# A Fourier filter and gated feed-forward kernel: the middle inverse stage with its operands exchanged, and its result passed on by crossbar transposes

## The chip, the cores and the metric

The kernel runs on one core of one Trainium2 chip. The core has five engines with queues of their own: TensorE (PE, with its weight loads listed apart as PEld), VectorE (DVE), ScalarE (ACT), GpSimd (POOL) and SyncE (SP, which here only issues DMAs). The metric is the time of one execution on the device in microseconds; lower is better. Several executions of one program are timed, and one more is profiled.

## The reference

The input x has 8 sequences of 3008 positions and 256 channels. Each sequence goes through a real Fourier transform along its positions, is multiplied by a complex filter for each frequency and channel, and is transformed back. The result, all 24064 rows of it, then goes through a feed-forward block: root-mean-square norm with a gain, two projections to 1536 columns, SiLU of one times the other, and a projection back to 256.

```python
X = np.fft.rfft(x, axis=1)
F = (filt_r + 1j * filt_i)[None, :, :]
y = np.fft.irfft(X * F, n=x.shape[1], axis=1)

rms = np.sqrt(np.mean(x * x, axis=-1, keepdims=True) + 1e-06)
xn = x / rms * rms_g
g = xn @ w_gate
silu = g * (1.0 / (1.0 + np.exp(-g)))
val = xn @ w_val
return (silu * val @ w_out).astype(np.float32)
```

Here `x` in the second part is y as rows of 256 channels. The output is float32; the kernel computes in fp16 with float32 sums.

## The kernel before

**The transform.** 3008 is 64 x 47, so the long transform is done in two stages each way, as small matrix products. Forward, stage A (`a_unit`) transforms over the 64 (n2), for two columns of n1 at a time; two halves of n1 (24 and 23 columns) lie in the two halves of the 128 partitions. Its result goes to DRAM (`z_store`, tensor z_tmp) and comes back with other axes on the partitions (`t2_load`). Stage B (`b_unit`) transforms over the 47, for two of the 32 values of k2 at a time. The product with the filter (lines 221, 241, 244 for batch 2 on; lines 234 and 235 for batches 0 and 1) gives tiles s of 128 frequencies' real and imaginary parts by 2 x 256 channels. From batch 2 on the two halves of the complex product are added on POOL (line 244) to one tile; in batches 0 and 1 two tiles are left, and the next matmul sums them.

**The middle inverse stage** is `bi_unit`: for each of the two k2, the matmul's stationary operand is a table wi of 128x128, the moving operand is s with 256 columns. It gives 96 useful rows (real and imaginary part for 48 columns of n1) on the partitions and channels along the free axis. ACT copies them to a tile t3 of four k2; `g_store` writes t3 to DRAM (g_tmp), and `t4_load` reads it back in four chunks of six n1 with 4 DMAs each, so that real and imaginary parts for 32 k2, and the two halves of n1, lie on the 128 partitions. 47 is odd: the last column of an even batch has only one half, so the odd batch after it takes the other half's row of the batch before (line 275), and both are computed together.

**The last stage** (`n_unit`) transforms over n2: the table wai is stationary, t4 moves. ACT copies the result and squares it (`sq_unit`), POOL makes the root (`stat_unit`) and scales (`xt_unit`), and `tr_unit` lays it out with channels on the partitions by a DMA transpose on SP's queue. Batch 0's first two groups of four columns take another way (`n_first`, `q_unit`, `scale_split`, `scale_apply`), with t4 as stationary operand.

**The feed-forward block.** For each batch there are 6 groups of 4 columns (512 rows; the last group of an even batch 3 columns), and for each group 12 slices of 128 hidden columns. `gv` makes four matmuls of 512 columns for a slice into the banks pg and pv, SiLU on ACT, the product on DVE; `down` makes four matmuls of 256 columns, two slots later.

**The order** is written out by hand, engine by engine in program order, by a table of slots: one slot is one `gv`, 72 slots a batch. `at(slot, ...)` places the units of the transforms of later batches between them. Batch 0's transform stands before the slots, in a loop of its own. For batch b of 3 on, with t = 72(b-1), `b_unit` i stands at t - 26 + 4i, `bi_unit` i at 8 slots later (`lag`), `t4_load` at t + 46 to t + 49, `n_unit` from t + 51 in steps of 4. Batch 1 has lag 3, loads at 53, rows from 55; batch 2 has lag 4, loads at 118, rows from 123. Each engine works its queue strictly in order, SP's queue of DMA issues included.

**PSUM.** The banks pg and pv are two each, po two; psa, psi and psn (lines 192, 253, 289) of batch 1 on share one bank (tag "mx"), psb has one. In batch 0 psi takes the pv banks.

**Buffers the change touches:** t3 (2 buffers), t4 (4), xt (2), sq (2), the table wi.

Of the kernel before, what the change touches and what calls it, by code (L numbers as in the profile page):

```python
# [11 lines left out]
FP16 = mybir.dt.float16  # L12
AXT = mybir.ActivationFunctionType
# [7 lines left out]
P = 128  # L21
D = 256
B = 8
DFF = 1536
JT = DFF // P
H = 24
K2 = 32
SL = 48
KR = 2 * SL
HALF = 64  # L30
S_INV_B = 0.25
S_INV_A = 0.25
# [6 lines left out]
def _make_tables():  # L39
# [18 lines left out]
    wb = np.zeros((KR, K2, P))  # L58
    wi = np.zeros((P, 1, 2, P))
    re, im = slice(0, N1), slice(SL, SL + N1)  # L60
# [36 lines left out]
    f = np.float16  # L97
    wi0 = wi[:, 0] * S_INV_B
    return wa.astype(f), (wai * S_INV_A).astype(f), wb.astype(f), wi0.astype(f), np.eye(P).astype(f)


@with_exitstack
def kernel(
# [12 lines left out]

    wa_np, wai_np, wb_np, wi0_np, id_np = _make_tables()
    wa_d = nc.inline_tensor(wa_np, name="wa_t").ap()
    wai_d = nc.inline_tensor(wai_np, name="wai_t").ap()
    wb_d = nc.inline_tensor(wb_np, name="wb_t").ap()  # L120
    wi0_d = nc.inline_tensor(wi0_np, name="wi0_t").ap()
    id_d = nc.inline_tensor(id_np, name="id_t").ap()

    z_d = nc.dram_tensor("z_tmp", (B, K2, KR, D), FP16, kind="Internal").ap()
    g_d = nc.dram_tensor("g_tmp", (B, K2, KR, D), FP16, kind="Internal").ap()

# [5 lines left out]
    ssp = ctx.enter_context(tc.tile_pool(name="ssp", bufs=3))  # L132
    t3p = ctx.enter_context(tc.tile_pool(name="t3p", bufs=2))
    t4p = ctx.enter_context(tc.tile_pool(name="t4p", bufs=4))
# [16 lines left out]
    wb = glob.tile([KR, K2, P], FP16)  # L151
    wi = glob.tile([P, K2, 2, P], FP16)
    fr = [glob.tile([P, KC, D], FP32, name="fr%d" % c) for c in range(K2 // KC)]
# [9 lines left out]

    st = {b: {"x": {}, "t1": {}, "t2": {}, "s": {}, "t3": {}, "t4": {}, "y": {}, "sq": {},
              "u": {}, "xn": {}} for b in range(B)}
# [81 lines left out]
    def bi_unit(b, i):  # L247
        ss = st[b]["s"].pop(i)
        ps = bank(0 if b else 2, "psi").rearrange("p (a d) -> p a d", a=2)
        n = len(ss)  # L250
        for u in range(2):
            for q in range(n):
                nc.tensor.matmul(ps[:, u, :], wi[:, 2 * i + u, q, :], ss[q][:, u, :],  # L253
                                 start=(q == 0), stop=(q == n - 1))
        c, r = divmod(i, 2)
        if r == 0:
            st[b]["t3"][c] = t3p.tile([KR, 4, D], FP16, tag="t3", name="t3")
        nc.scalar.activation(out=st[b]["t3"][c][:, 2 * r:2 * r + 2, :], in_=ps[0:KR], func=AXT.Copy)  # L258

    def g_store(b, c):  # L260
        nc.sync.dma_start(g_d[b, 4 * c:4 * c + 4, :, :].rearrange("k p d -> p k d"),
                          st[b]["t3"].pop(c))

    def t4_load(b, c):
        t = t4p.tile([P, XC, D], FP16, tag="t4", name="t4")
        w = XC - 1 if c == NXC - 1 else XC
        for h in range(2):
            for ri in range(2):
                p0 = h * 64 + ri * 32
                r0 = ri * SL + h * H + c * XC  # L270
                wh = XC if (b % 2 and not h) else w
                (nc.scalar if b == 0 and c == 0 and h else nc.sync).dma_start(
                    t[p0:p0 + 32, 0:wh, :], g_d[b, :, r0:r0 + wh, :])
                if wh < XC and b % 2:
                    nc.sync.dma_start(t[p0:p0 + 32, wh, :], g_d[b - 1, :, ri * SL + H - 1, :])
        st[b]["t4"][c] = t
# [51 lines left out]
    def n_first(m):  # L328
        y = yp.tile([P, 2, 512], FP32, tag="y", name="y")
        sq = sqp.tile([P, 2, 512], FP16, tag="sq", name="sq")  # L330
        for dh in range(2):
# [127 lines left out]
    def wi_group(g):  # L459

        ps = bank(1 + g % 2, "pst").rearrange("p (a d) -> p a d", a=4)
        lo = 1 if g == 0 else 0
        for a in range(lo, 4):
            nc.tensor.matmul(ps[:, a, :], wb[:, 4 * g + a, :], ident[0:KR, :], start=True, stop=True)
        k = slice(4 * g + lo, 4 * g + 4)
        nc.scalar.activation(out=wi[:, k, 0, :], in_=ps[:, lo:4, :], func=AXT.Copy, scale=S_INV_B)
        for p0 in (0, HALF):
            nc.vector.tensor_scalar(out=wi[p0:p0 + HALF, k, 1, :],
                                    in0=ps[HALF - p0:P - p0, lo:4, :], scalar1=S_INV_B,
                                    scalar2=None, op0=ALU.mult)  # L470
# [29 lines left out]
    with tc.manual_schedule():  # L500
# [3 lines left out]
        for c in range(NXC):  # L504
            x_load(0, c)
        nc.sync.dma_start(wa, wa_d)
        nc.sync.dma_start(ident, id_d)
        wb_load(0)
# [33 lines left out]
        for i in range(19):  # L542
# [9 lines left out]
            if i >= 3:  # L552
                bi_unit(0, i - 3)
                if i % 2 == 0:
                    g_store(0, i // 2 - 2)
            if i == 16:
# [36 lines left out]
        for b in range(1, B):  # L593
# [5 lines left out]
            elif b == 2:  # L599
                a_at = [22 + 2 * i for i in range(12)]  # L600
                b_at = [50 + 4 * i for i in range(16)]
                lag, t4_at, n_at = 4, 118, 123
            else:
# [9 lines left out]
            for i in range(16):  # L613
# [5 lines left out]
                at(s0 + lag, bi_unit, b, i)  # L619
                if i % 2 == 1:  # L620
                    at(s0 + lag + 1, g_store, b, i // 2)
            if b + 1 < B:
# [52 lines left out]
```

## Time and profile before

Three executions took 949.34 to 952.16 us, median 950.18. The profiled execution:

| what | value |
| --- | --- |
| its time | 950.33 us |
| its span, first to last instruction | 948.5 us |
| mean granted TensorE clock | 0.962 |
| matmuls po (line 415), 2256 | 343.5 us, 272 ns each |
| matmuls pg and pv (line 398), 2304 | 676.8 us, 375 ns each |
| matmuls psi (line 253), 320 | 272 ns each at full clock |
| ACT copies of psi (line 258), 128 | 75.6 us, 593 ns each |
| POOL sums s (line 244), 96 | 110.7 us, 1153 ns each |
| g_tmp stores, 64 of 192 KB | 2.7 us from issue to landing |
| g_tmp loads, 102 of 96 KB and 32 smaller | 3.5 us from issue to landing (the 96 KB ones) |
| DMA transposes (line 324), 46 | 3.1 us from issue to landing |

Busy times of PE overlap: matmuls are pipelined, so the time from one start to the next is less than a single one's duration, and the lines of a group add up to more than the span share that they hold. A line such as `L253 PE MATMUL psi<-s,wi` names the source line, the engine, the operation and output from inputs. "Idle before" is the time that the engine stood still ahead of an instruction, and the releaser is what ended it. SPq is SP's queue: its durations are those of issuing a DMA, not of moving the data.

### The profile page before, as it was taken

How to read it: one execution, taken by the hardware profiler on the slowest of the kernel's cores; microseconds unless marked ns; L12 is line 12 of the kernel's file. 1: busy time of each engine (PE TensorE's matmuls, PEld its weight loads, DVE VectorE, ACT ScalarE, POOL GpSimd, SP SyncE). 2: the span in 40 equal slices, each digit the busy share in tenths (PEclk: the TensorE clock that was granted, in tenths of full speed). 3: DMA queues.
4: the chain of work that ended last, by engine and by line, in shares of the span. 5: the costliest groups of instructions: out<-in, count | busy, mean ns of one | idle time of the engine just before them, and what ended most of it. 6: DMA issues, size and time to landing. Idle time of an engine off the chain costs nothing.

```text
span 948.5 us, 16157 instructions
## 1 busy us (share of the span) xinstructions
PE 868.2 (92%) x5403; PEld 529.4 (56%) x5403; DVE 664.5 (70%) x993; ACT 644.4 (68%) x1334; POOL 350.2 (37%) x383
## 2 busy tenths in 40 slices
PE   3354978999999999999999999999999999999997
PEld 1232545555555666666666666566666666565554
DVE  6632555677777888688877888788868888555554
ACT  7253767677766886688866886688757775677543
POOL 3485434335531544145422444044403443032100
PEclk9555999999999999999999999999999999999999
DMA  8968786764457534664457534743454423332201
GB/s 200 143 140 195 158 171 132 163 168 89 94 118 165 110 86 93 153 148 96 96 124 162 115 93 91 169 107 84 98 115 106 95 62 70 97 73 46 56 24 45
DMA packets 129075, 107.86 MB, mean 114 GB/s; under 512 B 57496, under 2 KB 108824, under 8 KB 128800
## 3 DMA queue, kind: packets, MB, share of 16 engines
q1 hardware_dynamic: 120112, 87.30, 39.5%
q0 software_dynamic: 8784, 19.34, 12.5%
q8 instruction: 42, 0.69, 0.3%
q14 instruction: 41, 0.34, 0.1%
q10 hardware_dynamic: 96, 0.20, 0.1%
HBM read 58.30 MB, written 49.81 MB: 114 GB/s over the span
## 4 chain that ended last, share of the span: by engine, by line
PE 74%; DMA 7%; DVE 6%; issue 4%; POOL 4%; ACT 3%; SPq 1%; ACTq 0%; POOLq 0%; DVEq 0%
PE po L415 22%; PE pg L398 22%; PE pv L398 21%; PE psi L253 3%; DVE hh L403 3%; DMA g_tmp<-t 3%; PE psb L213 2%; PE psn L289 2%; POOL s L244 2%; PE psa L192 2%; DVE s L241 2%; DMA fi<-in_filt_i_dram 2%; DVE o L421 1%; ACT sg L402 1%; DMA xc<-in_x_dram 1%
## 5 line engine op out<-in xcount | busy, mean ns | idle before, releaser
L403 DVE TENSOR_TENSOR hh<-pv,sg 128x512 f16<-128x512 f32 (+1 forms) x576 | 391.5, 680 | 219.4 <-ACT sg L402 109.5
L402 ACT ACTIVATE sg<-pg 128x512 f16<-128x512 f32 (+1 forms) x576 | 337.2, 586 | 210.9 <-PE pg L398 207.9
L415 PE MATMUL po<-wo,hh 128*128 128x256 f16 x2256 | 343.5, 272 | 2.5 <-DVE o L421 0.7
L398 PE MATMUL pg<-xn,wg 128*128 128x512 f16 (+1 forms) x1152 | 338.4, 375 | 0.0
L398 PE MATMUL pv<-xn,wv 128*128 128x512 f16 (+1 forms) x1152 | 338.4, 375 | 0.0
L415 PEld LDWEIGHTS <-hh 128*128 128x128 f16 x2256 | 219.9, 98 | 131.1 <-issue 11.9
L244 POOL TENSOR_TENSOR s<-s,s 128x512 f16<-128x512 f16 x96 | 110.7, 1153 | 375.2 <-DVE s L241 330.0
L398 PEld LDWEIGHTS <-wv 128*128 128x128 f16 x1152 | 112.9, 98 | 131.4 <-issue 1.1
L241 DVE TENSOR_TENSOR s<-psb,fi 64x512 f16<-64x512 f32 x192 | 132.3, 689 | 5.9
L398 PEld LDWEIGHTS <-wg 128*128 128x128 f16 x1152 | 112.7, 98 | 14.6 <-issue 1.5
L258 ACT ACTIVATE t<-psi 96x512 f16<-96x512 f32 x128 | 75.6, 593 | 28.3 <-PE psi L253 14.6
L315 POOL TENSOR_TENSOR xt<-y,rho 128x1024 f16<-128x1024 f32 (+1 forms) x46 | 85.4, 1858 | 3.6
L297 ACT ACTIVATE junk<-y 128x256 f16<-128x256 f32 x180 | 74.2, 412 | 3.0
L253 PEld LDWEIGHTS <-wi 128*128 128x128 f16 x320 | 32.9, 105 | 63.5 <-issue 28.8
L221 DVE TENSOR_TENSOR s<-psb,fr 128x512 f16<-128x512 f32 x96 | 65.5, 682 | 2.6 <-PE psb L213 2.1
L194 ACT ACTIVATE t<-psa 128x512 f16<-128x512 f32 x96 | 56.3, 600 | 9.2 <-PE psa L192 7.1
L213 PE MATMUL psb<-t,wb 96*128 96x256 f16 x256 | 52.1, 288 | 9.1 <-DMA t<-z_tmp 8.0
L291 ACT ACTIVATE y<-psn 128x512 f32<-128x512 f32 x92 | 54.2, 589 | 7.6 <-PE psn L289 0.8
L253 PE MATMUL psi<-s,wi 128*128 128x256 f16 x256 | 46.2, 272 | 8.0 <-POOL s L244 5.8
L192 PE MATMUL psa<-xc,wa 128*128 128x512 f16 x96 | 36.7, 397 | 14.8 <-DMA xc<-in_x_dram 9.4
L307 POOL TENSOR_TENSOR rho<-u,mhalf 128x4 f32<-128x4 f32 (+1 forms) x46 | 46.5, 1010 | 3.8
L176 POOL DMA_DIRECT2D xc<-in_x_dram x64 | 35.4, 562 | 13.2 <-PE psa L192 6.2
(64 smaller groups left out, 378.9 us busy)
## 6 DMA issues: line engine op xcount, KB each, us to landing
out_dram<-o SPq DMA_DIRECT2D x84, 256.0 KB, 3.3
z_tmp<-t SPq DMA_DIRECT2D x128, 96.0 KB, 2.1
t<-z_tmp SPq DMA_DIRECT2D x32, 384.0 KB, 5.1
g_tmp<-t SPq DMA_DIRECT2D x64, 192.0 KB, 2.7
xc<-in_x_dram POOLq DMA_DIRECT2D x56, 192.0 KB, 5.0
t<-g_tmp SPq DMA_DIRECT2D x102, 96.0 KB, 3.5
out_dram<-o SPq DMA_DIRECT2D x12, 192.0 KB, 3.0
t<-g_tmp SPq DMA_DIRECT2D x24, 80.0 KB, 2.2
```

The lines of the kernel that those rows point to most:

```text
L213: nc.tensor.matmul(ps[:, u, :], wb[:, k, :], st[b]["t2"][k // KC][:, k % KC, :], start=True, stop=True)
L221: nc.vector.tensor_tensor(out=s1, in0=ps, in1=f1, op=ALU.mult)
L241: nc.vector.tensor_tensor(out=s2[a], in0=ps[e], in1=f2[e], op=ALU.mult)
L244: nc.gpsimd.tensor_tensor(out=s, in0=s1, in1=s2, op=ALU.add)
L253: nc.tensor.matmul(ps[:, u, :], wi[:, 2 * i + u, q, :], ss[q][:, u, :], start=(q == 0), stop=(q == n - 1))
L258: nc.scalar.activation(out=st[b]["t3"][c][:, 2 * r:2 * r + 2, :], in_=ps[0:KR], func=AXT.Copy)
L297: nc.scalar.activation(out=junk, in_=y[:, i, ts(u, D)], func=AXT.Square, accum_out=ss[:, 2 * i + u:2 * i + u + 1])
L315: nc.gpsimd.tensor_tensor(out=xt[:, 0:n, :], in0=y.rearrange("p a (u d) -> p (a u) d", u=2)[:, 0:n, :], in1=rho[:, 0:n].unsqueeze(2).to_br ...
L398: nc.tensor.matmul(ps[:, 0:w], wt[:, dt_, ts(jt, P)], xn[:, 0:nq(b, m), dt_, :], start=(dt_ == 0), stop=(dt_ == 1))
L402: nc.scalar.activation(out=sg[:, 0:w], in_=pg[:, 0:w], func=AXT.Silu)
L403: nc.vector.tensor_tensor(out=hh[:, 0:w], in0=pv[:, 0:w], in1=sg[:, 0:w], op=ALU.mult)
L415: nc.tensor.matmul(po[s4 // 2][:, s4 % 2, :], hh[:, ts(s4, P)], wo[:, jt, :], start=(jt == 0 and s4 % 2 == 0), stop=(jt == JT - 1 and (s4 ...
```

## The change

In `bi_unit` the operands are exchanged: the product s is now stationary, in blocks of 128 channels, and the table moves, cut to its 96 useful columns. The result has channels on the partitions and the 96 rows along the free axis. The table's columns are put into the order (n1 within its half, half of n1, real or imaginary), by a permutation matrix in the matmul that makes the table. ACT copies the result to one tile `uu`, which holds a whole batch: 128 channels x 2 blocks x 24 columns x (4 parts x 32 k2). `t4_load` then is a pair of DMA transposes for each chunk, from uu to t4, on SP's queue. t3, `g_store`, g_tmp and their DMAs go. The half column of an even batch is kept in a small tile `left` by a POOL copy, and put into uu for the odd batch by another. Batch 2's lag goes from 4 to 8. The tile sq of batch 0's first groups moves into the buffers of xt.

```diff
-    wi = np.zeros((P, 1, 2, P))
+    wi = np.zeros((P, 1, 2, KR))
...
+    r = np.arange(KR)
+    perm = np.zeros((KR, KR))
+    perm[r, (r % H) * 4 + (r % SL // H) * 2 + r // SL] = 1.0
+    wi0 = (wi[:, 0] * S_INV_B) @ perm
...
-    wi = glob.tile([P, K2, 2, P], FP16)
+    perm = glob.tile([KR, KR], FP16)
+    wi = glob.tile([P, K2, 2, KR], FP16)
+    uu = glob.tile([P, 2, H, P], FP16)
+    left = glob.tile([P, 2, HALF], FP16)
...
     def bi_unit(b, i):
         ss = st[b]["s"].pop(i)
-        ps = bank(0 if b else 2, "psi").rearrange("p (a d) -> p a d", a=2)
+        ps = bank(0 if b else 2, "psi")[:, 0:4 * KR].rearrange("p (h u j) -> p h u j", h=2, u=2)
         n = len(ss)
-        for u in range(2):
-            for q in range(n):
-                nc.tensor.matmul(ps[:, u, :], wi[:, 2 * i + u, q, :], ss[q][:, u, :],
-                                 start=(q == 0), stop=(q == n - 1))
-        c, r = divmod(i, 2)
-        if r == 0:
-            st[b]["t3"][c] = t3p.tile([KR, 4, D], FP16, tag="t3", name="t3")
-        nc.scalar.activation(out=st[b]["t3"][c][:, 2 * r:2 * r + 2, :], in_=ps[0:KR], func=AXT.Copy)
-
-    def g_store(b, c):
-        nc.sync.dma_start(g_d[b, 4 * c:4 * c + 4, :, :].rearrange("k p d -> p k d"),
-                          st[b]["t3"].pop(c))
+        for dh in range(2):
+            for u in range(2):
+                for q in range(n):
+                    nc.tensor.matmul(ps[:, dh, u, :], ss[q][:, u, ds(dh * P, P)],
+                                     wi[:, 2 * i + u, q, :], start=(q == 0), stop=(q == n - 1))
+        dst = uu.rearrange("p h c (r k) -> p h k (c r)", r=4)[:, :, 2 * i:2 * i + 2, :]
+        nc.scalar.activation(out=dst, in_=ps, func=AXT.Copy)
+        if i == K2 // 2 - 1:
+            if b % 2:
+                nc.gpsimd.tensor_copy(out=uu[:, :, H - 1, HALF:P], in_=left)
+            else:
+                nc.gpsimd.tensor_copy(out=left, in_=uu[:, :, H - 1, 0:HALF])
 
     def t4_load(b, c):
         t = t4p.tile([P, XC, D], FP16, tag="t4", name="t4")
-        w = XC - 1 if c == NXC - 1 else XC
-        for h in range(2):
-            for ri in range(2):
-                p0 = h * 64 + ri * 32
-                r0 = ri * SL + h * H + c * XC
-                wh = XC if (b % 2 and not h) else w
-                (nc.scalar if b == 0 and c == 0 and h else nc.sync).dma_start(
-                    t[p0:p0 + 32, 0:wh, :], g_d[b, :, r0:r0 + wh, :])
-                if wh < XC and b % 2:
-                    nc.sync.dma_start(t[p0:p0 + 32, wh, :], g_d[b - 1, :, ri * SL + H - 1, :])
+        w = XC - 1 if (c == NXC - 1 and b % 2 == 0) else XC
+        for dh in range(2):
+            nc.sync.dma_start_transpose(t[:, 0:w, ds(dh * P, P)],
+                                        uu[:, dh, c * XC:c * XC + w, :].rearrange("p c t -> p (c t)"))
         st[b]["t4"][c] = t
...
-        sq = sqp.tile([P, 2, 512], FP16, tag="sq", name="sq")
+        sq = xtp.tile([P, 4, D], FP16, tag="xt", name="sq").rearrange("p (a e) d -> p a (e d)", a=2)
...
-        ps = bank(1 + g % 2, "pst").rearrange("p (a d) -> p a d", a=4)
+        ps = bank(1 + g % 2, "pst")[:, 0:4 * KR].rearrange("p (a d) -> p a d", a=4)
...
-            nc.tensor.matmul(ps[:, a, :], wb[:, 4 * g + a, :], ident[0:KR, :], start=True, stop=True)
+            nc.tensor.matmul(ps[:, a, :], wb[:, 4 * g + a, :], perm, start=True, stop=True)
...
+        nc.sync.dma_start(perm, pm_d)
...
-                if i % 2 == 0:
-                    g_store(0, i // 2 - 2)
...
-                lag, t4_at, n_at = 4, 118, 123
+                lag, t4_at, n_at = 8, 118, 123
...
-                if i % 2 == 1:
-                    at(s0 + lag + 1, g_store, b, i // 2)
```

More of the change, by code (lines that the diff above doesn't have):

```diff
@@ L97, in _make_tables @@
     f = np.float16
-    wi0 = wi[:, 0] * S_INV_B
-    return wa.astype(f), (wai * S_INV_A).astype(f), wb.astype(f), wi0.astype(f), np.eye(P).astype(f)
+    r = np.arange(KR)
+    perm = np.zeros((KR, KR))
+    perm[r, (r % H) * 4 + (r % SL // H) * 2 + r // SL] = 1.0
+    wi0 = (wi[:, 0] * S_INV_B) @ perm
+    return wa.astype(f), (wai * S_INV_A).astype(f), wb.astype(f), wi0.astype(f), np.eye(P).astype(f), perm.astype(f)
 @with_exitstack
@@ L115 @@
     nc = tc.nc
-    wa_np, wai_np, wb_np, wi0_np, id_np = _make_tables()
+    wa_np, wai_np, wb_np, wi0_np, id_np, pm_np = _make_tables()
     wa_d = nc.inline_tensor(wa_np, name="wa_t").ap()
@@ L122 @@
     id_d = nc.inline_tensor(id_np, name="id_t").ap()
+    pm_d = nc.inline_tensor(pm_np, name="pm_t").ap()
     z_d = nc.dram_tensor("z_tmp", (B, K2, KR, D), FP16, kind="Internal").ap()
-    g_d = nc.dram_tensor("g_tmp", (B, K2, KR, D), FP16, kind="Internal").ap()
     glob = ctx.enter_context(tc.tile_pool(name="glob", bufs=1))
@@ L132 @@
     ssp = ctx.enter_context(tc.tile_pool(name="ssp", bufs=3))
-    t3p = ctx.enter_context(tc.tile_pool(name="t3p", bufs=2))
     t4p = ctx.enter_context(tc.tile_pool(name="t4p", bufs=4))
@@ L161 @@
     mhalf = glob.tile([P, 4], FP32)
-    st = {b: {"x": {}, "t1": {}, "t2": {}, "s": {}, "t3": {}, "t4": {}, "y": {}, "sq": {},
+    st = {b: {"x": {}, "t1": {}, "t2": {}, "s": {}, "t4": {}, "y": {}, "sq": {},
               "u": {}, "xn": {}} for b in range(B)}
```

## The prediction

> **What bounds the kernel now.** I read the page's busy shares, then busy time by stretch, then TensorE's waits, then the chain of waits over the first 100 us. The page and four stretches (columns: stretch, length, busy time and count of PE, PEld, DVE, ACT, POOL, granted clock, DMA share, GB/s):
>
> ```profile
> PE 868.2 (92%) x5403; PEld 529.4 (56%) x5403; DVE 664.5 (70%) x993; ACT 644.4 (68%) x1334; POOL 350.2 (37%) x383
> ...
> 30.00:72.00 42.00, 20.34 (x90) 11.86 (x90) 17.80 (x22) 17.59 (x25) 30.50 (x36) 0.54 0.76 135
> 72.00:91.00 19.00, 6.93 (x40) 4.04 (x41) 3.98 (x8) 4.31 (x8) 10.67 (x18) 0.50 0.80 203
> 91.00:200.00 109.00, 97.43 (x618) 59.00 (x617) 61.86 (x96) 77.81 (x156) 43.02 (x55) 1.00 0.78 163
> 200.00:300.00 100.00, 94.20 (x590) 57.43 (x589) 76.81 (x117) 69.75 (x151) 39.53 (x40) 1.00 0.53 115
> 300.00:400.00 100.00, 99.88 (x629) 61.23 (x627) 78.61 (x118) 75.01 (x159) 40.00 (x42) 1.00 0.54 113
> ```
>
> The 92% is an average of two regimes. From 300 us PE is busy 99.88 of 100 us: only PE's own work shortens that stretch. Before 91 us PE is at half clock and mostly idle. The stretch 200 to 300 has 5.8 us of PE idle, which the waits name (total us, times, longest):
>
> ```profile
> PE psi L253 <- POOL s L244: 5.8, 13, 0.8
> PE psa L192 <- ACT t L258: 3.8, 7, 0.7
> ```
>
> The first hundred microseconds are a chain in which the bounce through g_tmp stands four times (start, duration, what):
>
> ```profile
> 49.20 6.54 DMA g_tmp<-t
> ...
> 59.08 6.12 DMA g_tmp<-t
> ...
> 65.30 0.60 ACT t L258
> ...
> 71.00 2.27 DMA g_tmp<-t
> ...
> 73.74 6.28 DMA t<-g_tmp
> ...
> 80.15 0.60 PE psn L335 x4
> ```
>
> At 49.20 and 59.08 a copy on ACT waits for an older store to land, as t3 has two buffers; at 71.00 to 80.02 the last store and first load stand between the last copy of batch 0 and its first row transform.
>
> **A. The matmuls of the middle stage.** Before: 320, of 256 columns. After: 640 of 96 columns, each with a weight load of its own (the products are now the loaded side). Batches 2 to 7 have 96 units of 2, now 4; batch 1 has 16 units of 4, now 8; batch 0 lies in the start and is counted in C. What a pair of weight load and short matmul costs at full clock stands in rows of other lines, start to start:
>
> ```profile
> 91.03 0.34 PE L352 MATMUL psq<-ones,sq 128*128 128x1 f16 x8
> 91.23 0.59 PE L398 MATMUL pg<-xn,wg 128*128 128x512 f16 x2
> ...
> 98.00 0.56 PE L380 MATMUL psr<-ident,hl 128*128 128x128 f16 x7 [0.27 <-DVE hl L371]
> 98.40 0.60 PE L415 MATMUL po<-wo,hh 128*128 128x256 f16 x4
> ...
> 601.61 0.38 PE L253 MATMUL psi<-s,wi 128*128 128x256 f16 x2
> 601.82 0.60 PE L415 MATMUL po<-wo,hh 128*128 128x256 f16 x4
> ```
>
> Eight pairs of one column take 0.20 us, 25 ns each: so a 128x128 load need not cost more than 25 ns. Seven pairs of 128 columns take 0.40 us, 57 ns each; two of 256 take 0.21 us. From 57 to 105 ns is 48 ns for 128 columns, 0.375 to 0.41 ns a column, so 96 columns give 43 to 45 ns. I take 43. Old: 96 x 0.21 + 16 x 0.42 = 26.9 us. New: 512 pairs x 0.043 = 22.0 us. A = -4.9. Bounds: 40 ns (0.41 x 96 alone) gives -6.4; 57 ns, as if 96 columns saved nothing against 128, gives +2.3.
>
> [...]
>
> **B. Batch 2's lag from 4 to 8 slots.** The 13 waits of psi for the sum s on POOL fall between 192 and 286 us, in batch 2, which alone has lag 4 in this form; batches 3 to 7 have lag 8 and show none. B = -5.8, with bounds 0 (another engine takes the wait; DVE is 77 to 79% busy there and at 300 to 400, where PE has no gap) and -5.8. Its last unit moves to slot 118, where the loads of t4 are issued; see D.
>
> **C. The start, batch 0.** Two steps. (1) With t3 gone, the two ACT waits vanish (4.72 and 4.04 us of ACT idle before 55.84 and 65.30). Not all of it is gained. In the first, the filter slice for the same queue is in flight anyway: its copy on ACT starts at 56.53, 0.7 us after. Two stores of 192 KB no longer compete with it, so perhaps 1.2 us. After the second, POOL idles 2.39 us before its last pair of products at 67.01; without the wait POOL runs on: 2.4. Together -3.6. (2) From the last copy's end (70.99) to the first row transform (80.15) are 9.2 us. In its place two transposes on SP's queue. The transposes that the kernel has:
>
> ```profile
> L324 SPq DMA_TRANSPOSE xn<-xt x46: 1232/1262/2055, 103.3 to 883.1; - x46
> ...
> DMA to landing us min/median/max: 3.0/3.1/6.3
> ```
>
> (ns to issue, min/median/max, then us from issue to landing.) Issue takes 1.25 us also for the few with six blocks, so I price the new ones alike. First half of the chunk lands after 3.1, the second after 1.25 + 3.1 = 4.4, plus 0.4 for the weight load that is in flight beside them: 4.8. Step -4.4. C = -8.0. Bounds: -2.5, if step 1 gives 0.9 (waits shifted to the filter slices) and the second transpose lands at the row's 6.3 (7.6 in place of 9.2); -15 if both ACT waits (8.8) and 9.2 - 3.1 = 6.1 are gained whole. What follows (root on POOL, weight slices, x of batch 1) hangs on this point in the same order, by DMAs that POOL issues after it, so I let the gain stand. Nearest to the middle: POOL-bound and DMA-bound steps remain.
>
> **D. The steady side of the transposes, SP's queue and the buffer uu.** Removed for each batch: 8 stores (about 0.32 us of issue each) and 16 or 18 loads; the timeline has "289.82 9.11" for 16 on SP's queue. Added: 8 transposes x 1.25 = 10.0 us. SP is not fuller, and first data come sooner: two issues (2.5) + 1.9 = 4.4 us after the last copy, against a store's 2.7 and then the loads. Behind them on SP stand output stores and z stores, which slip by about 1 us into buffers that are next needed slots later. uu has one buffer: the first copy of the next batch waits on ACT until all eight have landed, 10.0 + 1.9 = 11.9 us. From the last copy's end to the next batch's first copy the timeline gives 16.6 us for batches 2 to 6 (393.46 to 410.06 for batch 3): no wait, also with 1.2 us of t2 loads ahead. Two places are tight. Batch 1 to 2: SP is free of the output store at 187.6, 10.0 of transposes plus 1.9 of z stores between them plus 1.9 to land: 201.4, while the new lag puts ACT's copy at 199.25. Behind that copy stand silu, and on PE the psn at 200.57, which needs the same PSUM bank: it gets it at 201.9 instead, 1.3 late. Batch 2 to 3: the last copy, now at slot 118, ends about 292.8, landing 304.7, copy due at 303.77, 0.9 late of which 0.7 is slack before the psn at 305.10: 0.2. D = +1.5, bounds 0 and +6 (every batch 1 us late).
>
> **E. Copies on ACT.** 128 were 96x512 at 593 ns; now 128x384, as the 128x384 form of L402 takes 486. Seven psa waits for that copy shorten by 0.1: E = -0.7. But the copy now writes fp16 64 bytes apart, which no row shows; 486 is the lower bound. Estimate of the upper: the two forms of L402 give 0.85 ns an element and 160 ns fixed, four times per element is 1.46 us. Elsewhere ACT is 75% busy and the copy ends at 410.65, the bank's next user starts at 411.38, so up to 593 + 730 = 1.32 us is hidden; 1.46 costs 0.14 x about 72 such places = +10. I take 486 (all writes of ACT seen run at one rate).
>
> The small POOL copies (8) lie in POOL's idle 60%; if that cover were gone they cost one short POOL operation each, about 0.2 us as the L305 form, 1.6 in all. The permutation's table is one 0.4 us issue ahead of the first z store, while SP waits for ACT.
>
> **Sum.** -4.9 - 5.8 - 8.0 + 1.5 - 0.7 = -17.9. The profiled execution's span is 948.5: 930.6. Its time was 950.33, 1.8 more than the span, and 0.15 above the median of 950.18: 932.4, said as 932.
>
> **Rivals.** (1) The start gives little (C at -2.5): the filter and weight transfers decide it anyway. For: DMA is 76 to 80% busy there. Against: four steps of the chain name g_tmp. 938. (2) Slower: PE's weight load becomes the bound. If a load cannot run under the matmul before it, a pair costs what the PEld rows show, 98 ns: 512 x 0.098 = 50.2, A = +23.3 instead of -4.9: 932.4 + 28.2 = 960.6. It decides from (26.9 + 13.0) / 512 = 78 ns a pair. For: every short matmul now has a load of 98 ns and 40 ns to hide it. Against: the 25 and 57 ns rows, where loads of the same size follow each other faster. (3) ACT's scattered copy is slow, 1.46 us: 932.4 + 10.7 = 943. Nothing in the profile speaks for or against. (4) The change does not remove the bounce: excluded, as g_tmp is gone from the program; but uu's single buffer could hold ACT in each batch: D at +6, 937.
>
> **Numbers.** Forecast 0.66, start gives little 0.12, uu holds ACT 0.07, slow copy 0.07, weight load bound 0.08. The likeliest one's own range is 926 to 938 (A -6.4 to 0, C -12 to -5). To leave no more than 2 in 10 out, it reaches to 944: 924 to 944. A measurement tells 0.3%, 2.9 us, from no change; slower than that needs the weight load bound or a copy beyond 1.6 us: 0.09; within 0.3%: 0.03; faster 0.88.
>
> **What would show it.** A: a group of four psi from its start to the next po in 0.17 us (0.39 would be rival 2). B: no psi wait for POOL near 200 to 290. C: first gv at 79 to 80 instead of 87.6, and no g_tmp in the chain. D: an ACT copy waiting on a transpose near 199 less the start's gain, and nowhere after 310. E: copies near 486 ns. I am wrong if PE's idle moves to psn waiting on ACT's copies, or if the chain at the start ends in filter transfers at the same time as before.

## The result, and the profile after

The changed kernel takes 1019.06 us (median of 4 runs, 1015.35 to 1021.27) against 951.14 us for the kernel before in the same session: a ratio of 1.071, 95% interval 1.067 to 1.075. The forecast was 932, in a range of 924 to 944. The change makes the kernel 7% slower, and the forecast has the wrong sign.

The profiled execution took 1020.5 us, with a span of 1018.7: 70.2 us more than the 948.5 before, and 88.1 more than the 930.6 of the sum. Three views of the changed kernel answer to those shown before. The page's busy shares, and below them the line of the new copy (columns: instructions, busy us, mean ns, idle of the engine before them):

```profile
PE 880.1 (86%) x5723; PEld 530.4 (52%) x5723; DVE 659.5 (65%) x993; ACT 785.7 (77%) x1334; POOL 352.7 (35%) x391
...
L262 ACT ACTIVATE uu<-psi 128x384 f16<-128x384 f32 x128 | 236.6, 1876 | 10.5 <-DMA t<-uu 7.2
```

The copies that they replace have this line in the page of before:

```profile
L258 ACT ACTIVATE t<-psi 96x512 f16<-96x512 f32 x128 | 75.6, 593 | 28.3 <-PE psi L253 14.6
```

ACT is busy 141 us longer (644.4 before), and the copies account for all of it: their line has grown by 161 us, from 75.6 to 236.6. (Lines of ACT overlap: they add up to 689.1 us before and 882.9 now, against 644.4 and 785.7 busy, so the engine's busy time grows by less than the line.) The sum had 486 ns for each copy, with 1.46 us as the upper bound. The stretches (columns as before: stretch, length, busy time and count of PE, PEld, DVE, ACT, POOL, granted clock, DMA share, GB/s):

```profile
91.00:200.00 109.00, 86.04 (x537) 48.93 (x538) 46.87 (x74) 77.93 (x130) 43.02 (x57) 0.90 0.58 117
...
300.00:400.00 100.00, 93.03 (x600) 55.53 (x599) 72.56 (x110) 83.29 (x143) 36.73 (x39) 0.98 0.45 95
```

In 300 to 400 us, where PE had been busy 99.88 of 100 us, it is now busy 93.03, and it gets through 600 instructions of a kernel that has more of them (5723 against 5403), where it got through 629. Between 91 and 200 us it is idle for 23 of 109 us, and the granted clock has fallen from 1.00 to 0.90. Who PE waits for (total us, times, longest):

```profile
PE psn L288 <- ACT uu L262: 39.1, 69, 5.7
PE psi L259 <- ACT uu L262: 28.1, 16, 11.7
PE psa L197 <- ACT uu L262: 13.6, 9, 2.1
```

The wait of psi for s on POOL (5.8 us, 13 times) is gone, as forecast. Three kinds of matmul wait for the new copy. psn did not wait for the old one; psa waited 3.8 us, 7 times, as the prediction shows, and psi waited in the start:

```profile
PE psi L253 <- ACT t L258: 16.0, 5, 8.2
```

One steady unit of batch 3 shows how (timeline of the changed kernel: start, duration, instruction, and in brackets the idle time before it and what ended it):

```profile
406.18 0.33 PE L259 MATMUL psi<-wi,s 128*128 128x96 f16 x4
...
406.35 0.39 PE L218 MATMUL psb<-t,wb 96*128 96x256 f16 x2
...
406.55 1.86 ACT L262 ACTIVATE uu<-psi 128x384 f16<-128x384 f32 x1
...
407.44 0.59 PE L397 MATMUL pv<-xn,wv 128*128 128x512 f16 x2
...
408.46 0.27 PE L288 MATMUL psn<-t,wai 128*128 128x256 f16 x1 [0.42 <-ACT uu L262]
```

The four pairs of load and matmul take 0.17 us, from 406.18 to psb at 406.35, as the forecast had it. But the copy runs from 406.55 to 408.41. The next user of the same PSUM bank, psn, would follow pv at 408.04 and starts at 408.46. That is 0.42 us. Not every one of the 16 units of a batch has a psn close behind it: in a steady batch psn waits like this 11 times, 4.7 to 5.4 us in all.

### The profile page after: what moved, and what is told of

Its sections match the earlier page's. It is cut to its first block, busy times and chain, and to the rows that moved or that the text cites. A ratio compares the mean times of both kernels' runs of the same rounds, so it can differ in the third digit from the quotient of the medians.

```text
span 1018.7 us, 16521 instructions
## 1 busy us (share of the span) xinstructions
PE 880.1 (86%) x5723; PEld 530.4 (52%) x5723; DVE 659.5 (65%) x993; ACT 785.7 (77%) x1334; POOL 352.7 (35%) x391
## 3 DMA queue, kind: packets, MB, share of 16 engines
q0 software_dynamic: 8784, 19.34, 11.6%
## 4 chain that ended last, share of the span: by engine, by line
PE 54%; ACT 24%; DMA 7%; DVE 6%; issue 5%; SPq 2%; POOL 2%; ACTq 0%; DVEq 0%; POOLq 0%
PE po L414 17%; PE pg L397 17%; ACT uu L262 16%; PE pv L397 14%; ACT sg L401 5%; PE psn L288 3%; DVE hh L402 2%; SPq L273 2%; DMA t<-uu 2%; PE psa L197 2%; DMA fi<-in_filt_i_dram 2%; DVE s L246 2%; DVE o L420 1%; PE psi L259 1%; DMA xc<-in_x_dram 1%
## 5 line engine op out<-in xcount | busy, mean ns | idle before, releaser
L401 ACT ACTIVATE sg<-pg 128x512 f16<-128x512 f32 (+1 forms) x576 | 366.8, 638 | 154.9 <-PE pg L397 148.6
L397 PE MATMUL pg<-xn,wg 128*128 128x512 f16 (+1 forms) x1152 | 342.1, 379 | 0.0
L397 PE MATMUL pv<-xn,wv 128*128 128x512 f16 (+1 forms) x1152 | 341.9, 379 | 0.0
L262 ACT ACTIVATE uu<-psi 128x384 f16<-128x384 f32 x128 | 236.6, 1876 | 10.5 <-DMA t<-uu 7.2
L288 PE MATMUL psn<-t,wai 128*128 128x512 f16 x92 | 34.5, 374 | 39.1 <-ACT uu L262 39.1
L197 PE MATMUL psa<-xc,wa 128*128 128x512 f16 x96 | 38.1, 412 | 25.7 <-ACT uu L262 13.6
L259 PEld LDWEIGHTS <-s 128*128 128x128 f16 x512 | 34.2, 98 | 31.2 <-issue 6.7
L259 PE MATMUL psi<-wi,s 128*128 128x96 f16 x512 | 40.0, 206 | 3.3 <-ACT y L290 2.3
```

What stands on the lines that cost most here:

```text
L259: nc.tensor.matmul(ps[:, dh, u, :], ss[q][:, u, ds(dh * P, P)], wi[:, 2 * i + u, q, :], start=(q == 0), stop=(q == n - 1))
L262: nc.scalar.activation(out=dst, in_=ps, func=AXT.Copy)
L288: nc.tensor.matmul(ps[:, 0:w * D], wai, st[b]["t4"][n1p // XC][:, n1p % XC:n1p % XC + w, :], start=True, stop=True)
L397: nc.tensor.matmul(ps[:, 0:w], wt[:, dt_, ts(jt, P)], xn[:, 0:nq(b, m), dt_, :], start=(dt_ == 0), stop=(dt_ == 1))
L401: nc.scalar.activation(out=sg[:, 0:w], in_=pg[:, 0:w], func=AXT.Silu)
```

## The experiments

Ten kernels were run. "Unit" below is one call of bi_unit. The times before are those of the kernel before in the same session.

**1. Is it the distance of the writes?** Two kernels change where the copy puts its elements. The first changes nothing else and writes them side by side, 192 to a half, so what the transposes read is in another order:

```
-        dst = uu.rearrange("p h c (r k) -> p h k (c r)", r=4)[:, :, 2 * i:2 * i + 2, :]
-        nc.scalar.activation(out=dst, in_=ps, func=AXT.Copy)
+        dst = uu.rearrange("p h c t -> p h (c t)")[:, :, 4 * SL * i:4 * SL * (i + 1)]
+        nc.scalar.activation(out=dst, in_=ps.rearrange("p h u j -> p h (u j)"), func=AXT.Copy)
```

> The changed kernel with one thing different: each copy on ACT writes its 2 x 192 elements side by side into uu, where the changed kernel writes them 64 bytes apart (uu's order, and so the output, is then another one). Theory W (the distance between ACT's writes is the whole loss): the copy takes 486 to 500 ns in place of 1876, psn and psa no longer wait for it (39.1 and 13.6 us), and the time comes to where the prediction's other steps put it, 928 to 942. Rival R (the copy is slow on its reading side, or by being a short form that follows four short matmuls): it stays at 1.8 us and the time at 1019. Rival T (transposes, the single uu and the start cost the time, the copy only adds to it): copy near 490 ns, but the time stays above 955.

Measured: 938.63 us (935.97 to 940.38), ratio 0.986 (0.984 to 0.989); the copy takes 491 ns. The slow copy is the whole of the slowdown. This kernel flatters the change a little, though: its output is not the reference's, and each unit now fills a piece of uu that only one chunk's transposes read, so the first transpose starts at 49.9 us, during batch 0's middle stage, and no copy waits for uu later.

The second keeps the result as it is and changes the order of the rows that the transposes make, with the table wai, the tile left and the order in the PSUM bank changed to match, so that the copy writes runs of eight elements (16 bytes):

```
+    wai = wai.reshape(4, K2, P).transpose(1, 0, 2).reshape(P, P)
...
-        dst = uu.rearrange("p h c (r k) -> p h k (c r)", r=4)[:, :, 2 * i:2 * i + 2, :]
+        dst = uu.rearrange("p h c (k r) -> p (h c) k r", r=4)[:, :, 2 * i:2 * i + 2, :]
...
```

> The changed kernel with t4's partitions in the order k2, half, part (and the rows of wai to match), so that the two k2 of a unit give 8 neighbours of 2 bytes in uu; the matmuls write the bank in the order k2, channel block. One copy now writes 48 runs of 16 bytes; it reads PSUM in runs of 4. The output is the reference's. Theory W: a run costs like one or two far writes, 160 ns + 48 x 4.5 ns and 336 x 0.85 ns near ones, 0.5 to 0.7 us a copy, and the time 928 to 945, faster than both. If each element pays for itself whatever its neighbour, 1.8 us and 1015 to 1022. If the broken reading of PSUM is what costs, above 1 us and 960 or more.

Measured: 941.05 us (938.97 to 941.59), ratio 0.989 (0.986 to 0.991); copy 491 ns.

**2. How does the price depend on the step?** The copy takes nine forms in turn, one for each unit number modulo nine:

```
+        v = i % 9
+        if v == 0:
+            nc.scalar.activation(out=flat[:, :, 0:192], in_=src, func=AXT.Copy)
...
+        elif v == 5:
+            nc.scalar.activation(out=flat.rearrange("p h (j s) -> p h s j", s=32)[:, :, 0:2, :], in_=ps, func=AXT.Copy)
+        elif v == 6:
+            nc.scalar.activation(out=flat.rearrange("p h (g s) -> p h g s", s=32)[:, :, :, 0:2], in_=src.rearrange("p h (g e) -> p h g e", e=2), func=AXT.Copy)
...
```

> The changed kernel with nine forms of the copy in turn, all 384 elements of fp16 from the same bank: one element every 2, 4, 8, 16, 32 and 64 bytes, and runs of 2, 4 and 8 elements every 64 bytes (uu's contents, and so the output, are others; uu is set to zero once at the start). [...] If the distance matters in steps: rising from 4 to 64 bytes.

Measured (mean ns of the 384 elements): side by side 491; one element every 4 bytes 604, 8 bytes 1033, 16 bytes 1886, 32 bytes 1812, 64 bytes 1858; runs of two, four and eight elements, 64 bytes apart, 496, 491 and 492. Three of the lines (8 bytes, 16 bytes, runs of two):

```profile
L269 ACT ACTIVATE uu<-psi 128x384 f16<-128x384 f32 x16 | 16.5, 1033 | 1.9 <-PE psi L259 1.8
L271 ACT ACTIVATE uu<-psi 128x384 f16<-128x384 f32 x16 | 30.2, 1886 | 1.0 <-PE psi L259 0.5
L277 ACT ACTIVATE uu<-psi 128x384 f16<-128x384 f32 x16 | 7.9, 496 | 0.9 <-PE psi L259 0.5
```

The price rises up to a step of 16 bytes (1886) and then stays (1812 and 1858); and two neighbours written together, 64 bytes apart, cost next to nothing extra (496 against 491). A "line" below is a stretch of 16 bytes, named for this step.

**3. The smallest repair.** The layout of the change stays, and only the copy's walk is turned: the inner loop goes over the two neighbouring k2 of a unit. The two blocks of the PSUM bank are ordered to match.

```
...
-        dst = uu.rearrange("p h c (r k) -> p h k (c r)", r=4)[:, :, 2 * i:2 * i + 2, :]
-        nc.scalar.activation(out=dst, in_=ps, func=AXT.Copy)
+        dst = uu.rearrange("p h c (r k) -> p (h c r) k", r=4)[:, :, 2 * i:2 * i + 2]
+        nc.scalar.activation(out=dst, in_=ps.rearrange("p u h j -> p (h j) u"), func=AXT.Copy)
```

> The changed kernel, uu's layout and all tables untouched; only the order in which a copy walks is turned: its inner loop goes over the unit's two k2, which are neighbours in uu, so it writes 192 pairs of 4 bytes, 64 bytes apart, instead of 384 single elements of 2 bytes, 64 bytes apart (the matmuls write the bank in the order k2, channel block, so that the walk has three dimensions). The output is the reference's. Theory S (a lone 2-byte write is what costs, not the distance): copy 490 to 500 ns, time 938 to 942 as with runs of 8. Rival L (a price for every 16-byte line that is entered): 192 lines, half the extra, about 1.0 to 1.2 us a copy, and PE waits little for it, 945 to 955.

Measured: 941.03 us (940.4 to 941.28), ratio 0.989 (0.987 to 0.991); copy 497 ns. With the same elements in the same places of uu, the order of the walk decides 78 us. The rival's price for each 16-byte line, whatever is written there, would have left this copy at 1.0 to 1.2 us; it falls here. This kernel is "the repaired change" below: what the change would have been with the copy as cheap as forecast. Its page, the line of its copy, and PE's waits for that copy:

```profile
PE 861.4 (92%) x5723; PEld 529.1 (56%) x5723; DVE 661.2 (70%) x993; ACT 631.6 (67%) x1334; POOL 351.2 (37%) x391
...
L262 ACT ACTIVATE uu<-psi 128x384 f16<-128x384 f32 x128 | 63.5, 497 | 13.2 <-PE psi L259 5.8 <-DMA t<-uu 4.7 <-PE pg L397 1.4
...
PE psi L259 <- ACT uu L262: 15.9, 3, 10.7
PE psn L288 <- ACT uu L262: 4.2, 2, 3.8
PE psa L197 <- ACT uu L262: 3.1, 7, 0.7
```

Its span is 938.6 us, 80.1 below that of the change. PE is busy 18.7 us less (861.4 against 880.1, for the same instructions), so 61.4 us of the slowdown were idle time of PE. The 18.7 are only in part a lower clock (a mean of 0.946 against 0.955). In the four stretches of 72 slots from slot 144 to 432 both kernels have a granted clock of 1.00, and the change is still busier by 1.8 us in each (103.65 against 101.86 us in the first). An estimate from the rows of that stretch: two pv are busy for 0.59 us ahead of a gap (the row at 407.44 above), and count 0.43 where the next matmul follows them (409.43 to 409.86); 0.16 us at each of psn's 11 waits is 1.8 us.

**4. What the write pays for.** Two kernels with nothing but copies in them. The first has twelve forms on three engines:

```
+        lone = flat.rearrange("p h (j s) -> p h j s", s=32)
+            nc.scalar.activation(out=lone[:, :, :, 1:3], in_=src.rearrange("p h (j k) -> p h j k", k=2), func=AXT.Copy)
+            nc.scalar.activation(out=lone[:, :, 0:64, 0:3], in_=src.rearrange("p h (j k) -> p h j k", k=3), func=AXT.Copy)
...
+            nc.vector.tensor_copy(out=flat.rearrange("p h (j s) -> p h s j", s=32)[:, :, 0:2, :], in_=src.rearrange("p h (u j) -> p h u j", u=2))
...
+            nc.gpsimd.tensor_copy(out=flat.rearrange("p h (j s) -> p h s j", s=32)[:, :, 0:2, :], in_=sb.rearrange("p h (u j) -> p h u j", u=2))
```

> Only durations count here: a kernel that leaves all of the computation out, loads one tile, forms one product in PSUM and copies 384 elements a partition in twelve forms, eight times over. Twelve forms in turn, fp16 unless said, from PSUM unless said: ScalarE side by side; lone elements 64 B apart; pairs of neighbours 64 B apart; the same pairs shifted by one element, so that each straddles two 4-byte words; runs of three 64 B apart; lone fp32 elements 64 B apart; lone fp16 elements 64 B apart read from SBUF; VectorE side by side, lone, pairs; GpSimd side by side and lone, from SBUF. In the kernel the first three took 491, 1876 and 497 ns. Theory S (a lone 2-byte element costs a read and a write of the word around it): shifted pairs like lone ones, 1.8 us, since no word is whole; runs of three 0.9 to 1.2 us, since every third element is half a word; lone fp32 490 to 500, since a whole word is written; read from SBUF slow as well. Theory P (any run of two or more elements heals it, whole words or not): shifted pairs 495, runs of three 495, lone fp32 1.85 us. Theory E (it is ScalarE alone): VectorE's lone form within 20% of its side-by-side one; if the memory sets it, VectorE's lone form over 1.3 us too.

Six of the groups by line and shape (busy us, mean ns). Line 152 is the lone form on POOL, 138 on ACT, 148 on DVE; 141 pairs shifted by one element, 143 lone fp32, 142 runs of three, all on ACT:

```profile
L152 POOL COPY uu<-xh 128x384 f16<-128x384 f16 x8 | 14.8, 1850 | 0.5
L138 ACT ACTIVATE uu<-pt 128x384 f16<-128x384 f32 x8 | 14.7, 1834 | 0.3
L148 DVE CAST uu<-pt 128x384 f16<-128x384 f32 x8 | 14.6, 1821 | 0.3
L141 ACT ACTIVATE uu<-pt 128x384 f16<-128x384 f32 x8 | 8.0, 1004 | 0.3
L143 ACT ACTIVATE uu<-pt 128x384 f32<-128x384 f32 x8 | 6.5, 811 | 0.3
L142 ACT ACTIVATE uu<-pt 128x384 f16<-128x384 f32 x8 | 5.8, 727 | 0.3
```

Side by side the three engines take 491 (ACT), 558 (DVE) and 508 ns (POOL); pairs on ACT take 492, and lone elements read from SBUF 1866. So three engines and two sources agree within 3% on the lone form (1821 to 1866): it is not ACT alone and not PSUM, and what these forms share is the write into SBUF. Theory E falls, and none of the others has all of the rest. Runs of three cost 727 and not 495, against P. Shifted pairs are slow, as a price of half words wants (1004, where 1.8 us was expected), but lone fp32 elements, all whole words, cost 811 and not 491. So a price for each 16-byte line that the walk enters was taken up again, this time with two rates: a dear one where half of a 4-byte word is written, a cheap one for whole words. The second kernel puts this to the test with eight new forms:

```
+            nc.scalar.activation(out=flat.rearrange("p h (j s) -> p h j s", s=4)[:, :, 0:96, 1:3], in_=by2, func=AXT.Copy)
+            nc.scalar.activation(out=lone[:, :, 0:96, 7:9], in_=by2, func=AXT.Copy)
...
+            nc.scalar.activation(out=lone[:, :, 0:48, 5:9], in_=src.rearrange("p h (j k) -> p h j k", k=4), func=AXT.Copy)
```

> Only durations count here; all of the computation is left out, and ScalarE copies 384 elements a partition from PSUM in eight forms, eight times over. What the forms so far fit: an instruction costs some 90 ns and then either 1.04 ns for each element or the price of its pieces, whichever is longer, where a piece is a 16-byte line of SBUF that the walk enters: some 4.7 ns if it writes a 2-byte half of a 4-byte word there, some 2 ns if it writes whole words only (theory L2). Its rival counts runs, not lines: 4.7 ns for each run of neighbours with a half word in it, wherever the run lies (theory R); another counts half words in any place (theory H: some 1.3 to 3.5 ns each over 491). Forms in turn: (1) side by side, shifted by one element (two half words in all): 491 to 500 by all. (2) shifted pairs 16 B apart: 990 to 1010 by L2 and R. (3) shifted pairs 8 B apart, two in a line: 540 to 600 by L2, 990 by R, 1000 by H. (4) pairs 64 B apart that straddle two lines: 1.8 to 1.9 us by L2, 1.0 us by R and H. (5) lone fp32 8 B apart, two in a line: 491 by L2; 811 if each whole word has its price. (6) lone fp32 16 B apart: 811. (7) runs of four 64 B apart that straddle two lines at a word's edge: 491. (8) runs of four that straddle two lines with half a word at either end: 990 by L2, 540 to 560 by R, 750 by H.

Six of the groups; the forms (1) to (8) are lines 138 to 145. Forms (1) and (7) took 497 and 492 ns:

```profile
L141 ACT ACTIVATE uu<-pt 128x384 f16<-128x384 f32 x8 | 14.0, 1756 | 0.0
L139 ACT ACTIVATE uu<-pt 128x384 f16<-128x384 f32 x8 | 8.2, 1020 | 0.3
L145 ACT ACTIVATE uu<-pt 128x384 f16<-128x384 f32 x8 | 7.8, 972 | 0.3
L143 ACT ACTIVATE uu<-pt 128x384 f32<-128x384 f32 x8 | 6.7, 843 | 0.3
L140 ACT ACTIVATE uu<-pt 128x384 f16<-128x384 f32 x8 | 4.8, 597 | 0.3
L142 ACT ACTIVATE uu<-pt 128x384 f32<-128x384 f32 x8 | 4.1, 507 | 0.3
```

All eight lie where L2 put them, or within 4% of it. Forms (2) to (6) and (8), in this order, took 1020, 597, 1756, 507, 843 and 972 ns. The forms that tell it from its rivals are (3), two shifted pairs in one line (597, against the 1020 of form 2 with the same number of pairs), (4), pairs across the edge of two lines (1756 against 1004 within one), and (8), 972. The two constants on record were a little off. Through 1834 ns for 384 lines, 1004 for 192 and 727 for 128 goes a line of 183 ns plus 4.3 ns for each line entered with a half word in it; it gives 596 for the 597 of form 3 and 1009 for the 1033 of experiment 2. For whole words, 811 and 843 ns over 384 lines give 1.6 and 1.7 ns a line; 507 ns over 192 lines fits that, but lies too near the 491 of side by side to tell. These are fits of durations; what the memory does inside was not seen.

Told by the step, without the fit: for fp16, against the 491 of side by side, a step of 2 elements costs 604, one of 4 costs 1033 and one of 8 costs 1886; two elements in a line take 492 when they make a whole word and 1004 when they don't. For fp32, a step of 2 elements takes 507 and one of 4 takes 843.

**5. What of the forecast's gains is real?** The kernel before with batch 2's lag raised, first to 7, then to 8 with its t4 loads one slot later:

```
-                lag, t4_at, n_at = 4, 118, 123
+                lag, t4_at, n_at = 7, 118, 123
```

> The kernel before with batch 2's lag at 7 slots in place of 4, nothing else (8 would put the last store behind the loads of t4 in this kernel). Step B of the prediction: the 13 waits of psi for POOL's sum between 192 and 286 us, 5.8 us, vanish, and the time falls by 4 to 6 us, to 944 to 946. Rival: the waits pass to another engine or to the loads at slot 118, and the time stays within 1.5 us of before.

Measured: 951.62 us (950.18 to 953.2), ratio 1.0004 (0.9991 to 1.0018): a miss. The wait for POOL is gone, but psa's wait for ACT's copy t rises from 3.8 us (7 times) to 11.6 (18 times), since with lag 7 psi falls into the slots of psa, which uses the same PSUM bank.

```
-                lag, t4_at, n_at = 4, 118, 123
+                lag, t4_at, n_at = 8, 119, 123
```

> The kernel before with batch 2's lag at 8 as in the change, and its loads of t4 one slot later (119) so that they stand behind the last store. With lag 7 the 5.8 us of psi waiting for POOL went, and 7.8 us of psa waiting for ACT's copy of psi came, as psi then shares its slot with psa of batch 3 and both use one bank. With lag 8 psi stands one slot behind psa and one ahead of psn. If that clash was the reason: 944 to 947. If batch 2's stretch is bound otherwise: within 1.5 us of before.

Measured: 942.85 us (942.53 to 946.33), ratio 0.992 (0.990 to 0.994). The lag alone gives most of what the repaired change gives; their intervals overlap, so what the exchange of the operands adds to the lag is not shown clear of noise.

**6. The start.** In the repaired change, the chain of waits (start, duration, what) shows where the start's gain went:

```profile
52.35 6.25 DMA fi<-in_filt_i_dram
...
70.05 0.51 ACT uu L262
70.58 1.32 SPq L273
71.95 6.54 DMA t<-uu
78.54 0.62 PE psn L334 x4
...
85.17 5.63 DMA ws<-in_moe_w_val_dram
...
94.81 0.56 PE psr L379 x7
```

The filter slice has taken the place of the bounce in the first part; the second transpose lands 6.54 us after its issue, where 3.1 + 0.4 had been taken, while the second weight slice is loaded; and a weight slice stands ahead of psr, the last step before the steady work. Two kernels pull at this. One issues the second weight slice only when the first transposes have landed:

```
-                w_load(1)
...
         gate(st[0]["t4"][0][0:1, 0, 0:1])
+        gate(st[0]["t4"][0][0:1, 0, P:P + 1])
+        w_load(1)
```

> pairs with the second third of the feed-forward weights asked for only after the first chunk of t4 has landed (in pairs it is asked for just before, and the two share the DMA engines: the second transpose lands 8 us after its issue, not 4.4). Theory K (step C failed as the transposes lose the DMA engines to the weights): the first row transform comes 3 to 5 us sooner, at 74 to 76 us. Whether that reaches the end is the question: if t4 sets the start, 2 to 5 us below pairs; if the weights' own chain does (each third is asked for when the one before has been scaled), within 1.5 us of pairs, or later, with the wait moved to the slots 4 to 12.

Measured: 940.7 us (940.62 to 941.12), ratio 0.989 (0.987 to 0.992). The second transpose lands 2.82 us after its issue, so the weight slice was what delayed it, and the first silu comes at 82.8 instead of 86.6 us; but psr starts at 94.50 instead of 94.81, and by slot 8 the gain is gone (98.6 against 98.9). The chain of this kernel shows the weight slices twice:

```profile
71.72 2.82 DMA t<-uu
...
75.61 7.45 DMA ws<-in_moe_w_val_dram
...
85.25 5.48 DMA ws<-in_moe_w_val_dram
...
92.69 1.06 POOL rho L357
```

The rho of group 1 stands on POOL's queue behind loads of x, and two of these start only as the third weight slice lands, at 91.01 and 92.11. Whether the 3.8 us would hold with these loads of x moved was not tried.

The other kernel issues batch 1's eight transposes from uu three slots earlier (t4_at 53 to 50), to shorten the wait for uu:

```
-                lag, t4_at, n_at = 3, 53, 55
+                lag, t4_at, n_at = 3, 50, 55
```

> pairs with batch 1's eight transposes at slots 50 to 53 in place of 53 to 56 (its rows stay at 55). Step D: the single uu makes the first copy of batch 2 wait for the last of these transposes, 4 us of PE in one place. Ahead of an output store and of the z stores of slot 54 they should end some 3.5 us sooner: 2.5 to 4 us below pairs. Rival: the transposes start no sooner, as they wait for the last copy of batch 1 and POOL's, and the time is that of pairs within 1.

Measured: 940.55 us (938.47 to 944.0), ratio 0.989 (0.986 to 0.992): the wait for uu falls from 3.8 to 2.3 us, less than expected, and the time does not tell it from the repaired change. The four versions with a cheap copy and the reference's output (941.05, 941.03, 940.7 and 940.55 us) cannot be told apart.

## Why the prediction was wrong, step by step

**E, ACT's copies: the failed step.** The copy was taken at 486 ns, with 1.46 us as the upper bound; it takes 1876. The mechanism was named as rival (3), with a chance of 0.07, and the sentence "slower than that needs the weight load bound or a copy beyond 1.6 us" says rightly what happened, as does the sign "PE's idle moves to psn waiting on ACT's copies". The reason given for 486, "all writes of ACT seen run at one rate", does not reach this copy, as no row had writes of lone fp16 elements apart. The upper bound was no bound: "four times per element" is a guess at a factor, for which the profile had no row. By the fit above this copy is 183 + 384 x 4.3 = 1834 ns, and the same 384 elements walked in pairs take 497.

With the right duration the step's own formula still gives too little: 1.88 us is 0.56 above what is hidden, times 72 places is 40 us, against 80. The 40 are about what psn's waits come to (39.1 us, 69 times). Left out were psa, which waits 10.5 us more than in the repaired change (13.6 against 3.1), psi, which waits 12.2 more (28.1 against 15.9), most of it in the start, and the 18.7 us that PE is busier. By the start of slots 0, 20, 72 and 144, the change is behind the repaired one by 9.5, 10.7, 35.1 and 46.1 us, and after that by 7 to 8 more in each of the next four batches' stretches and 4 in the last. So the start loses 10, where copies stand in the chain one behind the other, and batch 1 loses 24, where they come almost every slot and psa and psn both queue for the bank. What the lower clock costs of this is not shown: in the other three executions of the change its mean was 0.985, 0.954 and 0.990, with spans of 1019.5, 1013.6 and 1015.9 us.

**A, the matmuls: right.** 0.17 us for four pairs is 42 ns a pair, against 43 assumed, and the repaired change takes 0.7 us less than before for each of the 72-slot stretches from 144 to 432. Rival (2), the weight load as the bound, is excluded by the same row.

**B, batch 2's lag: right in mechanism, too small.** -5.8 was forecast; the lag alone takes 7.1 us off the span (948.5 to 941.4): PE is busy 2.3 us less (868.2 against 865.9), besides the waits that are gone. It needed the right slot: with a lag of 7 the prediction's bound of 0, another wait in the place of this one, is what came.

**C, the start: mis-sized, -3 in place of -8, inside its bounds.** In the repaired change psr starts at 94.81 instead of 98.00. Step (1) was to give 3.6: the last copy of batch 0 ends at 70.56 instead of 70.99, so 0.4. The bound of the prediction, waits shifted to the filter slices, is what the chain shows. Step (2) was to give 4.4: from the last copy to the psn of the second half, at 78.54, are now 8.0 us instead of 9.2, so 1.2 (the first half's psn starts at 73.47), as the second transpose takes 6.54 us to land beside the weight slice. The row's longest, 6.3 us, was in the bounds. The 0.4 us taken for the weight slice was the author's estimate, and no row showed it: without the slice beside it the transpose lands in 2.82 us, so the slice costs 3.7. Rival (1), "the start gives little", was right as far as it went. And "I let the gain stand" was wrong too: with 3.8 us gained at slot 0, the weights take it back.

**D, uu's single buffer: right place, too small.** The wait was forecast at batch 1 to 2 with 1.3 us and at batch 2 to 3 with 0.2; in the repaired change it is 3.8 and 0.4, and nowhere later, so rival (4), a wait in each batch, is excluded. But it costs more than it lasts. Windows of the repaired change around it, columns as above:

```profile
195.00:200.00 5.00, 1.21 (x6) 0.40 (x4) 0.76 (x2) 0.83 (x2) 0.00 (x0) 0.81 0.83 191
200.00:205.00 5.00, 5.00 (x21) 2.80 (x20) 2.96 (x5) 2.63 (x8) 1.11 (x1) 0.50 0.01 2
205.00:210.00 5.00, 5.00 (x40) 3.48 (x39) 4.47 (x8) 4.45 (x12) 3.17 (x4) 1.00 0.50 120
```

From 190 to 195 us PE finished 37 instructions at a clock of 1.00. After a gap of 3.79 us the clock is at 0.50 for a whole 5 us, in which PE gets through 21 instructions instead of 40, though it is busy throughout: by estimate 2.5 us more. D is then 3.8 + 0.4 + 2.5 = 6.7 us, above its upper bound of 6.

**The sum, mended.** Repaired change: A about -5.4 (512 pairs of 42 ns against 26.9), B -7.1, C -3.2, D +6.7, E without the slow copy -0.7 as forecast (psa's 3.8 us of waiting fell to 3.1): -9.7, against 938.6 - 948.5 = -9.9. That is closer than the terms are known, as executions of one kernel lie 1 us and more apart. The change itself adds 80.1 for the copy. So the forecast would have been too low even with the copy at its 486 ns: the repaired change's 941 lies outside the likeliest range of 926 to 938.

## What to carry to other kernels

Before a copy is priced by its element count, look at what its innermost loop writes: fp16 elements one at a time and apart cost here up to 3.8 times the same elements written in pairs (1876 against 497 ns), and a turn of the loop order can be the whole repair. A cost that no row shows has no upper bound that can be made by multiplying a row; there the chance of the bad case belongs with the size it would have, and the break-even duration (here 1.6 us) says how near it is. And a gain at the start counts only up to the next transfer that everything waits for.

## What was not expected of the hardware

By the fit above, a lone 2-byte write by ACT costs 4.3 ns for each 16-byte line entered, and the 384 elements take about as long on DVE and POOL (1834, 1821 and 1850 ns). A whole word alone costs 1.6 to 1.7 ns (811 and 843 ns), and a pair that fills its word nothing beyond the element's time (492 ns, 491 side by side).

In the repaired change a gap on PE of 3.79 us was followed by 5 us at half clock. In the changed kernel one of 5.68 us, at 226.93, was followed by the same:

```profile
230.00:235.00 5.00, 2.39 (x9) 1.28 (x9) 1.38 (x2) 3.13 (x4) 0.00 (x0) 0.50 0.02 4
```

Shorter gaps did it too. In the changed kernel psa waited 2.09 us before it started at 150.48, and psn 2.28 us before 341.31. In the 3.4 us that hold each of these gaps PE was busy for 1.2 us, and the next 3.4 us ran at half clock, though PE was busy throughout:

```profile
148.00:151.31 3.31, 1.22 (x13) 0.79 (x10) 1.29 (x2) 2.81 (x6) 0.00 (x0) 1.00 1.09 229
151.31:154.73 3.42, 3.42 (x11) 1.52 (x10) 0.69 (x1) 0.91 (x3) 0.00 (x0) 0.50 0.69 131
...
339.05:342.46 3.41, 1.15 (x8) 0.75 (x8) 0.72 (x2) 2.85 (x3) 0.00 (x0) 1.00 0.82 170
342.46:345.88 3.42, 3.42 (x12) 1.50 (x11) 2.04 (x3) 2.10 (x6) 0.85 (x1) 0.50 0.57 208
```

The half clock lasted 3.42 us after each of these two, and 6.8 us (229.8 to 236.65) after the gap of 5.68. Gaps of about 1.7 us did not always do this. After those of 1.71 us before 195.91 and 1.72 us before 203.81 the clock stayed at 1.00; PE was busy for 1.70 us of 193.90 to 197.31 and 1.69 us of 202.00 to 205.40. One of 1.72 us before 188.76 did, with other gaps close before it (PE busy 0.82 us of 185.45 to 188.86, then 3.42 us at a clock of 0.50). From 130 to 345 us the clock of this kernel fell six times, at 137.66, 151.31, 158.14, 188.86, 229.82 and 342.46, each time at the end of 3.41 us in which PE was busy for 0.52 to 1.35 us; at 151.31, 188.86 and 342.46 no single gap was longer than 2.3 us.
